# Two loads swapped between queues, and layernorm block 2 moved ahead of block 0, in the opening of a one-core attention and gMLP kernel

## The chip, the cores and the metric

The kernel runs on one core of a Trainium2 chip. The metric is device time in microseconds of one execution, taken as the median of several runs. A profiled execution has a time of its own and a span: from the first recorded instruction to the last. The core's engines run at the same time and each works through its own instructions in order: TensorE (PE; its weight loads are listed as PEld), VectorE (DVE), ScalarE (ACT), GpSimd (POOL) and SyncE (SP, here only an issuer of DMAs). ScalarE and GpSimd issue DMAs too. An instruction that needs another engine's result, or a transfer, waits for a semaphore, and everything behind it on its engine waits with it.

## The reference

Input x has 2048 rows of 512 values. It is normalized row by row, and two branches use the result: A, attention in which each position looks at 8 earlier ones two apart, and B, a gated MLP whose gate half z2 is normalized once more and mixed over the rows. The output is x plus both.

```python
def _B_ref(x, w_in, w_sp, b_sp, w_out):
    z = _gelu(jnp.einsum('bsd,df->bsf', x, w_in))     # w_in: 512 x 1792
    z1 = z[..., :Fh].copy()                           # Fh = 896
    z2 = _layernorm(z[..., Fh:], axis=-1)
    g = jnp.einsum('ts,bsf->btf', w_sp, z2) + b_sp[None, :, None]
    return jnp.einsum('bsf,fd->bsd', z1 * g, w_out)
x = A_x
xn = _layernorm(x, axis=-1)
return x + _A_ref(xn, A_wqkv, A_wo) + _B_ref(xn, B_w_in, B_w_sp, B_b_sp, B_w_out)
```

Only the opening of the kernel matters here: loading the first blocks of x and the z2 half of w_in, normalizing those blocks, transposing them, and the first z2 products.

## The kernel before

x is cut into 16 blocks of 128 rows. Each block goes through `ln_block`: VectorE takes statistics (`bnst`, L616, then `bnag`, L619), GpSimd turns the variance into a reciprocal root (`rstd`, L621), VectorE normalizes (`norm`, L631). For blocks 0 to 3 TensorE then transposes the block in two halves (`xTr..a` and `xTr..b`, L647), and ScalarE copies each half from PSUM to SBUF (`xTe..a`, `xTe..b`, L654). Blocks 4 and up are transposed by DMAs issued from SyncE (`xTd`, L635).

Block 0 has a shorter way. It is only centred, the second half by VectorE (`ctr1`, L624) and the first by ScalarE (`ctr0`, L626); the centred halves are transposed and used for its z2 product, and rstd0 is applied as the scale of the gelu. The normalized block 0 (`norm0`) is transposed separately for later use: `xNr` on TensorE (four transposes, L667) and `xNe` on ScalarE (L671). The first later user is Q0_0, the first product of the attention branch.

`z2_block` multiplies a transposed block with the z2 half of w_in, in two column halves of 448 (named 0 and 1, from the weights w2a and w2b); each column half is a sum over four chunks of the 512 inner values. For blocks 0 to 3 the sum is split into two tasks of two matmuls, `a` for the inner half 0 and `b` for the inner half 1 (z2_1_0a is block 1, column half 0, inner half 0; L824). ScalarE applies the gelu (`z2g`, L835). After z2 of blocks 0 to 3 come Q and K (L700), V (L682) and the rest; the DVE works on attention products from 17 us on.

The weights of z2 come in four loads of 224 KB (`ld_win_h`, L557): ldw_in2a_0, ldw_in2a_1, ldw_in2b_0 and ldw_in2b_1, where the last digit is the inner half. Each block of x is a load of 128 KB (`ld_x`, L547). Three loads of 512 KB follow for Q, K and V (ldq, ldk, L571; ldwv, L579).

A planner orders the tasks of each engine, but the openings are written out by hand in `plan.orders` (from L1061): one list for VectorE, one for ScalarE, one for SyncE, one for TensorE. In these lists an engine follows the text exactly. The loads of the opening are issued from two queues: SyncE issues ldx0, ldx1, ldw_in2a_0, ldw_in2b_0, ldx3 and others, ScalarE issues ldw_in2a_1, ldw_in2b_1 and ldx2. The loads ldx4, ldx5, ldx6, ldx7, ldq and ldk wait until ldw_in2b_1 has landed (`reads=[("w_in2b", 1)]`, `after=`). While TensorE waits for data at the very start it runs 28 small matmuls on constants (`warm`, L588).

Of the kernel before, what the change touches and what calls it, by code (L numbers as in the profile page):

```python
# [14 lines left out]
class Plan:  # L15
# [300 lines left out]
    warm=28,  # L316
    fill0=1,
# [4 lines left out]
def build_kernel(nc, A_x, A_wqkv, A_wo, B_x, B_w_in, B_w_sp, B_b_sp, B_w_out, out, report=False, sched_kw=None,  # L322
# [79 lines left out]
    with ExitStack() as es:  # L402
# [10 lines left out]
        def A(name, n, o2_=0):  # L413
            return ar[:, off[name] + o2_: off[name] + o2_ + n]

        def AC(o_, dims):
            return bass.AP(tensor=ar, offset=o_, ap=[[AR, 128]] + [list(d) for d in dims])
# [93 lines left out]
        def dma(eng, fn, nbytes, chan, reads=(), writes=(), name="", xbar=False, prio=None, lat=1700.0):  # L511
            return T(eng, fn, reads=tuple(reads), writes=tuple(writes), name=name, prio=prio,
                     dma=dict(chan=chan, nbytes=nbytes, xbar=xbar, lat=lat))
# [23 lines left out]
        def setup_masks():  # L537
            T("pool", lambda g: g.memset(maskt, 0.0), reads=[("rstd", 3)], writes=["maskt"], est=150, name="mask0", prio=2)
            mv = maskt.rearrange("p (w h) -> p w h", w=8)
            T("pool", lambda g: g.affine_select(out=mv, in_=mv, pattern=[[-2, 8], [0, 32]], compare_op=ALU.is_ge,  # L540
                                                fill=NEG_BIG, base=0, channel_multiplier=1),
              writes=["maskt"], est=400, name="mask1", prio=2)

        def xin_ap(sl):
            return A("xin", 512, 512 * sl) if sl < 4 else A("xin2", 512, 512 * (sl - 4))

        def ld_x(b, eng="sp", after=()):  # L547
            sl = b % 8
            dma(eng, lambda e: e.dma_start(xin_ap(sl), x2[128 * b:128 * b + 128, :]), 128 * 512 * 2,  # L549
                ("xin", sl), reads=after, writes=[("xin", sl)], name="ldx%d" % b)  # L550

        def ld_win(nm, lo, n, eng, after=()):
            dma(eng, lambda e: e.dma_start(AC(off["w_in"] + lo, [[1792, 4], [1, n]]),
                                           B_w_in[:, lo: lo + n].rearrange("(c p) n -> p c n", p=128)),
                512 * n * 2, nm, reads=after, writes=[nm], name="ld" + nm)

        def ld_win_h(nm, lo, n):  # L557
            for h in range(2):
                dma(("sp", "act")[h], (lambda h: lambda e: e.dma_start(  # L559
                    AC(off["w_in"] + lo + 2 * 1792 * h, [[1792, 2], [1, n]]),  # L560
                    B_w_in[256 * h: 256 * h + 256, lo: lo + n].rearrange("(c p) n -> p c n", p=128)))(h),
                    256 * n * 2, (nm, h), writes=[(nm, h)], name="ld%s_%d" % (nm, h))

        ld_x(0)
        ld_x(1)
        ld_win_h("w_in2a", FH, HF)
        ld_win_h("w_in2b", FH + HF, HF)
        ld_x(2, "act")
        ld_x(3, "sp")
        for which, eng in ((0, "sp"), (1, "sp")):  # L570
            dma(eng, (lambda which: lambda e: e.dma_start(  # L571
                AC(off["wqk"] + 512 * which, [[1024, 4], [1, 512]]),
                A_wqkv[:, 512 * which: 512 * which + 512].rearrange("(c p) n -> p c n", p=128)))(which),
                512 * 512 * 2, ("wqk", which), reads=[("w_in2b", 1)],
                writes=[(("wq", "wk")[which], c) for c in range(4)],
                name="ld%s" % ("qk"[which]))
        for b in range(4, min(8, NB)):
            ld_x(b, "sp", after=[("w_in2b", 1)])
        dma("sp", lambda e: e.dma_start(A("wv_raw", 2048).rearrange("p (c n) -> p c n", c=4),  # L579
                                        A_wqkv[:, 1024:1536].rearrange("(c p) n -> p c n", p=128)),  # L580
            512 * 512 * 2, "wv", writes=["wv_raw"], name="ldwv")
# [93 lines left out]
        def v_block(b):  # L675
            k = next_bank()
            sl = b % 4

            def mm(t):
                last = None  # L680
                for dc in range(4):
                    last = t.matmul(bank(k), AC(off["xnT"] + dc * S + 128 * b, [[1, 128]]),  # L682
                                    AC(off["wv_raw"] + 512 * dc, [[1, 512]]), start=(dc == 0), stop=(dc == 3))
                return last
            T("pe", mm, reads=[("xnT", b), "wv_raw"], writes=[("ps", k)], est=4 * c_mm(512), name="V%d" % b)
            T("act", lambda a: a.activation(A("Vn", 512, 512 * sl).rearrange("p (d h) -> p d h", d=16),
                                            bank(k).rearrange("p (h d) -> p d h", d=16), ACTF.Copy),
              reads=[("ps", k)], writes=[("Vn", sl)], est=c_act(512), name="Ve%d" % b)
            dma("pool", lambda e: e.dma_start(vscr[16 + 128 * b: 16 + 128 * b + 128, :], A("Vn", 512, 512 * sl)),
                128 * 512 * 2, ("vwr", sl), reads=[("Vn", sl)], writes=[("vscr", b)], name="Vw%d" % b)  # L690
# [165 lines left out]
        def z2_sq(b):  # L856
            T("act", lambda a: a.activation(A("sqj", FH), A("z2", FH, FH * b), ACTF.Square, accum_out=Fv("s2", 1, b)),  # L857
              reads=[("z2h", b, 0), ("z2h", b, 1)] + ([("z2h", 3, 1)] if b < 4 else []), writes=["sqj", ("s2", b), ("z2", b)],
              est=c_act(FH, psum=False, accum=True), name="z2s%d" % b)
# [30 lines left out]
        for j in range(NJ):  # L890
            bl = range(4 * j, 4 * j + 4)
            for b in bl:
                if b >= 8:
                    ld_x(b)
            if j == 1:
                ld_win("w_in1", 0, FH, "sp")
            if j == 0:
                for fn_, b, k0 in ((ln_block, 0, 3), (ln_block, 1, 1), (z2_block, 0, 5), (xn0_T, 0, 3), (ln_block, 2, 3), (z2_block, 1, 7),
                                   (z2_block, 2, 1), (ln_block, 3, 3), (z2_block, 3, 3)):
                    ring[0] = k0  # L900
                    fn_(b)
                setup_masks()
                dma("pool", lambda e: e.dma_start(vscr[0:16, :], ar[0:16, off["zeros"]: off["zeros"] + 512]), 16 * 512 * 2,
                    ("vwr", 0), reads=["zeros"], writes=[("vscr", -1)], name="Vzero", prio=2)
                ring[0] = 5
            else:
                for b in bl:
                    ln_block(b)
            if j == 1:
                dma("sp", lambda e: e.dma_start(A("bbc", S), bass.AP(tensor=B_b_sp.tensor, offset=B_b_sp.offset,  # L910
                                                                     ap=[[0, 128], [1, S]])),
                    128 * S * 2, "bbc", writes=["bbc"], name="ldbbc")
            if j >= 1:
                for b in bl:
                    v_block(b)
            for c in range(4):
                qk_pair(j, c)
            if j == 0:
                for b in bl:
                    v_block(b)  # L920
            prod_reduce(j)
            softmax(j)
            if j >= 1:
                for b in bl:
                    z2_block(b)
                for b in range(4 * (j - 1), 4 * j):
                    z2_sq(b)
                z2_wave(j - 1)
# [129 lines left out]
        for q in qord:  # L1058
# [1 line left out]

        plan.orders = [  # L1061
            """
                bnst0 bnag0 ctr1 bnst1 bnag1 norm0 norm1 bnst2 bnag2 bnst3 norm2 bnag3 bnst4 norm3 bnag4 bnst5 norm4
                bnag5 bnst6 norm5 bnag6 bnst7 norm6 bnag7
            """.split(),
            """
                actprime ldw_in2a_1 ldw_in2b_1 ldx2 ctr0 xTe0b xTe0a xTe1a xTe1b xNe z2g0_0 xTe2a xTe2b z2g0_1 z2g1_0
                xTe3a xTe3b z2g1_1 z2g2_0 z2g2_1 z2g3_0 z2g3_1
            """.split(),
            """  # L1070
                ldx0 ldx1 ldw_in2a_0 ldw_in2b_0 ldx3 ldx4 ldx5 ldq ldk ldx6 ldx7 ldwv
            """.split(),
            """
                warm xTr0b fill0 xTr0a z2_0_0b z2_0_1b z2_0_0a xTr1a xTr1b z2_0_1a xNr z2_1_0a z2_1_0b z2_1_1a xTr2a
                xTr2b z2_1_1b z2_2_0a z2_2_0b xTr3a xTr3b z2_2_1a z2_2_1b z2_3_0a z2_3_0b z2_3_1a z2_3_1b Q0_0 K0_0 Q0_1
                K0_1 Q0_2 K0_2 Q0_3 K0_3 V0 V1 V2 V3 V4 V5 V6 V7 Q1_0 K1_0 Q1_1 K1_1 Q1_2 K1_2 Q1_3 K1_3 z2_4_0 z2_4_1
                z2_5_0 z2_5_1 z2_6_0 z2_6_1 z2_7_0 z2_7_1 V8 V9 V10 V11 Q2_0 K2_0 Q2_1 K2_1 Q2_2 K2_2 Q2_3 K2_3 z2_8_0
                z2_8_1 z2_9_0 z2_9_1 z2_10_0 z2_10_1 z2_11_0 z2_11_1 V12 V13 V14 V15 Q3_0 K3_0 Q3_1 K3_1 Q3_2 K3_2 Q3_3
# [99 lines left out]
```

## Time and profile before

| What | us |
|---|---|
| median of 3 runs (lowest, highest) | 235.45 (235.31, 235.59) |
| the profiled execution's own time | 236.14 |
| its span | 233.8 |
| TensorE busy in the span | 229.3 (98%) |
| VectorE busy | 202.3 (87%) |
| ScalarE busy | 119.1 (51%) |
| GpSimd busy | 51.7 (22%) |

Busy times add up what an engine's instructions took; they do not say which engine sets the end. For that one reads the chain that ended last, followed back from the last instruction. In a timeline, a bracket at the end of a line tells how long the engine had been idle before the instruction and what released it. DMAs are seen twice: as an issue on the queue of the engine that issues them (SPq, ACTq), and as packets on a hardware queue, q1 for those of SyncE and q10 for those of ScalarE.

### The profile page before, as it was taken

To read this page: it belongs to the slowest core of one execution; us is meant where nothing else is said; L and a number is where in the kernel's file an instruction comes from. 1 tells how busy PE (TensorE), PEld (TensorE's weight loads), DVE (VectorE), ACT (ScalarE), POOL (GpSimd) and SP (SyncE) were. 2 spreads that over 40 slices of the span, in tenths; PEclk is the share of its full clock that TensorE was granted. 3 is DMA by queue.
4 is the path that set the end of the run, shared out by engine and by line. 5 is a ranking of instruction groups with operands and counts; after the bars stand their busy time and mean duration, and the time that the engine had idled before them with its cause. 6 is when DMAs were issued, how large, how long until landed. Compare 5 with 4: busy or idle time off the path is not lost.

```text
span 233.8 us, 2996 instructions
## 1 busy us (share of the span) xinstructions
PE 229.3 (98%) x1108; PEld 112.7 (48%) x1127; DVE 202.3 (87%) x230; ACT 119.1 (51%) x235; POOL 51.7 (22%) x69
## 2 busy tenths in 40 slices
PE   8999999999999999999999999999999999999996
PEld 6554455554554444444444444444444444444544
DVE  4769979998989989997999998999999999999200
ACT  4789588989988978952021124341232415101442
POOL 4548964680780050001201000010000000000000
PEclk9999999999999999999999999999999999999999
DMA  6897850399909999681429999999829794920412
GB/s 220 271 251 173 188 139 3 103 196 330 353 32 179 216 238 267 121 231 51 141 78 276 252 167 246 229 323 292 265 53 260 138 251 108 227 44 7 112 48 67
DMA packets 87166, 41.76 MB, mean 179 GB/s; under 512 B 66272, under 2 KB 86000, under 8 KB 87152
## 3 DMA queue, kind: packets, MB, share of 16 engines
q1 hardware_dynamic: 71072, 23.24, 47.8%
q10 hardware_dynamic: 14640, 14.13, 21.0%
q0 software_dynamic: 1440, 4.21, 6.3%
q8 instruction: 9, 0.15, 0.3%
q14 instruction: 5, 0.04, 0.1%
HBM read 20.05 MB, written 5.26 MB: 108 GB/s over the span
## 4 chain that ended last, share of the span: by engine, by line
PE 96%; DMA 2%; issue 1%; SPq 1%; ACT 0%
PE ps L959 41%; PE ps L700 12%; PE ps L1029 10%; PE ps L847 10%; PE ps L824 10%; PE ps L1025 6%; PE ps L682 6%; DMA arena<-in_B_w_in_dram 2%; SPq L549 0%; PE ps L647 0%; SPq L559 0%; ACT arena L1038 0%; PE ps L667 0%
## 5 line engine op out<-in xcount | busy, mean ns | idle before, releaser
L959 PE MATMUL ps<-arena 128*128 128x512 bf16 x440 | 97.1, 379 | 0.4
L959 PEld LDWEIGHTS ps<-arena 128*128 128x128 bf16 x448 | 43.8, 98 | 52.8
L953 ACT ACTIVATE ps<-arena 128x512 f32<-128x512 bf16 x28 | 16.5, 599 | 48.5 <-DVE arena L966 47.8
L984 DVE TENSOR_TENSOR arena<-arena 128x4096 bf16<-128x4096 bf16 x16 | 36.3, 2284 | 0.4
L724 DVE TENSOR_TENSOR arena<-arena 128x4096 bf16<-128x4096 bf16 x16 | 36.1, 2280 | 0.1
L988 DVE TENSOR_TENSOR arena<-arena 128x4096 bf16<-128x4096 bf16 (+1 forms) x16 | 28.0, 1753 | 0.3
L700 PE MATMUL ps<-arena 128*128 128x512 bf16 x127 | 28.1, 379 | 0.1
L729 DVE TENSOR_TENSOR arena<-arena 128x4096 bf16<-128x4096 bf16 x12 | 27.4, 2287 | 0.2
L1029 PE MATMUL ps<-arena 128*128 128x512 bf16 (+2 forms) x123 | 26.8, 355 | 0.2
L824 PE MATMUL ps<-arena 128*128 128x448 bf16 x128 | 25.8, 353 | 0.3 <-ACT arena L654 0.2
L1038 ACT ACTIVATE arena<-ps 128x512 bf16<-128x512 f32 (+2 forms) x17 | 9.5, 561 | 29.6 <-PE ps L1029 29.6
L847 PE MATMUL ps<-arena 128*128 128x512 bf16 x109 | 24.0, 379 | 0.2
L700 PEld LDWEIGHTS ps<-arena 128*128 128x128 bf16 x128 | 14.5, 113 | 13.1
L966 DVE TENSOR_TENSOR arena<-ps,arena 128x512 bf16<-128x512 f32 x28 | 19.1, 681 | 0.6 <-PE ps L959 0.6
L1029 PEld LDWEIGHTS ps<-arena 128*128 128x128 bf16 x126 | 13.6, 113 | 11.0
L708 ACT ACTIVATE arena<-ps 128x1024 bf16<-128x1024 f32 x16 | 16.4, 1022 | 3.1 <-PE ps L700 2.5
L824 PEld LDWEIGHTS ps<-arena 128*128 128x128 bf16 x128 | 12.0, 98 | 11.9 <-ACT arena L654 1.2
L852 ACT ACTIVATE arena<-ps 128x512 bf16<-128x512 f32 x28 | 16.0, 595 | 3.2 <-PE ps L847 2.7
L835 ACT ACTIVATE arena<-ps 128x448 bf16<-128x448 f32 x30 | 16.2, 552 | 2.3 <-issue 0.3
L847 PEld LDWEIGHTS ps<-arena 128*128 128x128 bf16 x112 | 10.9, 98 | 13.2
L1025 PE MATMUL ps<-arena 128*128 128x512 bf16 (+2 forms) x71 | 16.7, 355 | 0.1
L857 ACT ACTIVATE arena<-arena 128x896 bf16<-128x896 bf16 x16 | 15.1, 944 | 0.0
(68 smaller groups left out, 195.5 us busy)
## 6 DMA issues: line engine op xcount, KB each, us to landing
arena<-vscr ACTq DMA_DIRECT2D x8, 1152.0 KB, 9.2
arena<-in_A_x_dram ACTq DMA_DIRECT2D x17, 128.0 KB, 5.9
vscr<-arena POOLq DMA_DIRECT2D x16, 128.0 KB, 2.5
arena<-in_A_x_dram SPq DMA_DIRECT2D x15, 128.0 KB, 2.9
out_dram<-arena ACTq DMA_DIRECT2D x15, 128.0 KB, 1.9
arena<-in_A_wqkv_dram SPq DMA_DIRECT2D x3, 512.0 KB, 5.8
ascr<-arena POOLq DMA_DIRECT2D x4, 256.0 KB, 5.1
arena<-ascr POOLq DMA_DIRECT2D x4, 256.0 KB, 4.0
```

Of the source, the lines that this page charges most:

```text
L700: last = t.matmul(bank(k + which), AC(off["wqk"] + 1024 * dc + col0, [[4, 128]]), AC(off["xnT"] + dc * S + 512 * j, [[1, 512]]), start=(dc ...
L724: T("dve", lambda v: v.tensor_tensor(pbv, qb, kb, ALU.mult), reads=[("QT", c, j), ("KT", c, j), ("KTpad", c, j)], writes=[("pb", s_)], est ...
L729: T("dve", lambda v: v.tensor_tensor(A("pb", 4096, 4096 * a), A("pb", 4096, 4096 * a), A("pb", 4096, 4096 * b), ALU.add), reads=[("pb", b) ...
L824: last = t.matmul(ps[:, 512 * k: 512 * k + HF], st, AC(off["w_in"] + 1792 * dc + c0, [[1, HF]]), start=(h == first and dc == 2 * h), stop= ...
L847: lastm = t.matmul(bank(k), AC(off["w_in"] + 1792 * dc + 128 * fc, [[1, 128]]), AC(off["xnT"] + dc * S + 512 * j, [[1, 512]]), start=(dc = ...
L953: T("act", lambda a: a.activation(bank(k), A("bbc", 512, 512 * tc), ACTF.Copy), reads=["bbc"], writes=[("ps", k)], est=c_act(512), name="g ...
L959: last = t.matmul(bank(k), AC(off["z2"] + FH * sh + 128 * fc, [[1, 128]]), AC(off["wT"] + WSL * r_ + sh * 512, [[1, 512]]), start=False, s ...
L966: T("dve", lambda v: v.tensor_tensor(uv, bank(k), uv, ALU.mult), reads=[("ps", k)], writes=[("z1T", fc, tc)], est=c_dve(512) + 20, name="u ...
L984: T("dve", (lambda iv, tv, av: lambda v: v.tensor_tensor(tv, iv, av, ALU.mult))(iv, tv, av), reads=[("attn", j), ("Ve", par)], writes=[("V ...
L988: T("dve", (lambda n: lambda v: v.tensor_tensor(AC(off["Vs"], [[4096, 2], [1, n]]), AC(off["Vs"], [[4096, 2], [1, n]]), AC(off["Vs"] + n, ...
L1025: t.matmul(po, AC(off["OT"] + 512 * ot_pos(tb) + 128 * cc, [[1, 128]]), AC(off["wo"] + 512 * cc + c0, [[1, n]]), start=False, stop=False, ...
L1029: last = t.matmul(po, AC(off["z1T"] + fc * S + t0, [[ts, 128]]), AC(off["w_out"] + 512 * fc + c0, [[1, n]]), start=False, stop=(fc == FC - ...
```

## The change

Three things change, all in the opening.

The loads: ldx1 moves from SyncE to the head of ScalarE's loads, and ldw_in2a_1 moves from there to the second place of SyncE's. The loads that waited for ldw_in2b_1 wait for ldw_in2a_0 instead.

VectorE's order: bnst2 moves ahead of norm1, norm2 ahead of bnst3, and norm0 from before norm1 to after bnag3.

TensorE's and ScalarE's order: the four transposes of the normalized block 0 (xNr) move from before z2_1 to before z2_3, and their copy (xNe) from before z2g0_0 to after z2g1_0. Some halves of z2_1 and the transposes of block 2 change places, and xNr gets another PSUM bank.

```diff
         def ld_win_h(nm, lo, n):
             for h in range(2):
-                dma(("sp", "act")[h], (lambda h: lambda e: e.dma_start(
+                dma("act" if h and nm == "w_in2b" else "sp", (lambda h: lambda e: e.dma_start(
...
         ld_x(0)
-        ld_x(1)
+        ld_x(1, "act")
...
-                512 * 512 * 2, ("wqk", which), reads=[("w_in2b", 1)],
+                512 * 512 * 2, ("wqk", which), reads=[("w_in2a", 0)],
...
-            ld_x(b, "sp", after=[("w_in2b", 1)])
+            ld_x(b, "sp", after=[("w_in2a", 0)])
...
-                for fn_, b, k0 in ((ln_block, 0, 3), (ln_block, 1, 1), (z2_block, 0, 5), (xn0_T, 0, 3), (ln_block, 2, 3), (z2_block, 1, 7),
+                for fn_, b, k0 in ((ln_block, 0, 3), (ln_block, 1, 1), (z2_block, 0, 5), (xn0_T, 0, 5), (z2_block, 1, 7), (ln_block, 2, 3),
...
-                bnst0 bnag0 ctr1 bnst1 bnag1 norm0 norm1 bnst2 bnag2 bnst3 norm2 bnag3 bnst4 norm3 bnag4 bnst5 norm4
+                bnst0 bnag0 ctr1 bnst1 bnag1 bnst2 norm1 bnag2 norm2 bnst3 bnag3 norm0 norm3 bnst4 bnag4 bnst5 norm4
...
-                actprime ldw_in2a_1 ldw_in2b_1 ldx2 ctr0 xTe0b xTe0a xTe1a xTe1b xNe z2g0_0 xTe2a xTe2b z2g0_1 z2g1_0
-                xTe3a xTe3b z2g1_1 z2g2_0 z2g2_1 z2g3_0 z2g3_1
+                actprime ldx1 ldw_in2b_1 ldx2 ctr0 xTe0b xTe0a xTe1a xTe1b z2g0_0 xTe2a xTe2b z2g0_1 xTe3a xTe3b z2g1_0
+                xNe z2g1_1 z2g2_0 z2g2_1 z2g3_0 z2g3_1
...
-                ldx0 ldx1 ldw_in2a_0 ldw_in2b_0 ldx3 ldx4 ldx5 ldq ldk ldx6 ldx7 ldwv
+                ldx0 ldw_in2a_1 ldw_in2a_0 ldw_in2b_0 ldx3 ldx4 ldx5 ldq ldk ldx6 ldx7 ldwv
...
-                warm xTr0b fill0 xTr0a z2_0_0b z2_0_1b z2_0_0a xTr1a xTr1b z2_0_1a xNr z2_1_0a z2_1_0b z2_1_1a xTr2a
-                xTr2b z2_1_1b z2_2_0a z2_2_0b xTr3a xTr3b z2_2_1a z2_2_1b z2_3_0a z2_3_0b z2_3_1a z2_3_1b Q0_0 K0_0 Q0_1
+                warm xTr0b fill0 xTr0a z2_0_0b z2_0_1b z2_0_0a xTr1a xTr1b z2_0_1a z2_1_0a z2_1_0b xTr2a xTr2b z2_1_1a
+                z2_1_1b z2_2_0a z2_2_0b xTr3a xTr3b z2_2_1a z2_2_1b xNr z2_3_0a z2_3_0b z2_3_1a z2_3_1b Q0_0 K0_0 Q0_1
```

## The prediction, made before the changed kernel ran

> **What bounds the kernel now.** I read the page first, then the chain that ended last from the start to 14 us, then the timelines of TensorE, VectorE and ScalarE up to 14 us, and last the DMA view in short stretches. Page and chain:
>
> ```profile
> span 233.8 us, 2996 instructions
> ...
> PE   8999999999999999999999999999999999999996
> ...
> PE 96%; DMA 2%; issue 1%; SPq 1%; ACT 0%
> ```
>
> ```profile
> 2.12 4.87 DMA arena<-in_B_w_in_dram
> 6.99 0.05 issue
> 7.04 0.55 PE ps L824 x2
> 7.59 0.22 PE ps L667 x4
> 7.81 1.14 PE ps L824 x6
> ```
>
> In the slices TensorE is full from the second to the last but one. In the chain everything after 7.04 us is matmul, with pieces of 0.05 us between: the rest of the span is a fixed queue of TensorE work of 224 us, and it can only start earlier or later. At 7.04 TensorE was waiting for a weight transfer issued at 2.12, which is w2b0 (ldw_in2b_0; w2a and w2b are the two column halves of the z2 weights, 0 and 1 their row halves; x0 to x7 are the blocks of x). So only the first 8 us can change the time, unless the change opens a hole later.
>
> What TensorE and ScalarE do there (start, length, engine, line):
>
> ```profile
> 5.37 1.37 PE L824 MATMUL ps<-arena 128*128 128x448 bf16 x6 [0.21 <-ACT arena L654]
> 6.58 0.39 PE L647 MATMUL ps<-arena 128*128 128x128 bf16 x4
> 6.89 0.66 ACT L654 ACTIVATE arena<-ps 128x256 bf16<-128x256 f32 x2 [1.29 <-PE ps L647]
> 7.04 0.55 PE L824 MATMUL ps<-arena 128*128 128x448 bf16 x2
> 7.42 0.39 PE L667 MATMUL ps<-arena 128*128 128x128 bf16 x4
> ```
>
> Six z2 matmuls at 0.19 us each (the chain's 1.14 for six) plus four transposes at 0.22 in all are 1.36 us of work, between 5.37 and 7.04. So 1.67 - 1.36 = 0.31 us of it is idle, and that is all that the loads and the order can win after 5.37 (0.13% of 235.45). The start at 5.37 hangs on x0 alone: landing, statistics at 3.19, centring at 4.16, transposes, copy.
>
> VectorE's order of the same time:
>
> ```profile
> 4.36 0.69 DVE L616 BATCH_NORM_STATS2 fpool<-arena 128x6 f32<-128x512 bf16 x1
> 5.08 0.20 DVE L619 BATCH_NORM_AGGREGATE fpool<-fpool 128x2 f32<-128x9 f32 x1
> 5.19 0.37 DVE L631 TENSOR_SCALAR arena<-arena,fpool 128x512 bf16<-128x512 bf16 x1
> 6.02 0.41 DVE L631 TENSOR_SCALAR arena<-arena,fpool 128x512 bf16<-128x512 bf16 x1 [0.46 <-POOL fpool L621]
> 6.42 0.69 DVE L616 BATCH_NORM_STATS2 fpool<-arena 128x6 f32<-128x512 bf16 x1
> ```
>
> These are bnst1, bnag1, norm0, norm1 (it waited 0.46 us for GpSimd's rstd1) and bnst2. The DMA view, cut to the issue of x2 and to two stretches of half a microsecond (2.75 to 3.25, and 5.5 to 6; queue, packets, MB):
>
> ```profile
> arena<-in_A_x_dram ACTq DMA_DIRECT2D x1, 128.0 KB, 4.5
> ```
>
> ```profile
> q10 hardware_dynamic: 177, 0.15, 90.2%
> q1 hardware_dynamic: 28, 0.03, 15.6%
> ```
>
> ```profile
> q1 hardware_dynamic: 204, 0.18, 102.6%
> q10 hardware_dynamic: 16, 0.01, 8.3%
> ```
>
> The first says that x2, issued at 1.87, landed 4.5 us later, at 6.37. Cutting the view around each issue gives the others: x0 issued 0.73, landed 3.1; w2a1 0.86, 3.8; x1 1.18, 4.1; w2b1 1.35, 5.65; w2a0 1.65, 6.05; x2 1.87, 6.37; w2b0 2.12, 7.0; x3 2.63, 7.3. The landings come in the order of issue over both queues, and in the two stretches one queue has nearly all the traffic although the other has a transfer waiting: x1, issued at 1.18 on SyncE's queue q1, hardly moves at 2.75 to 3.25, while ScalarE's q10 carries weights issued earlier.
>
> **The change part by part.** *The loads.* x1 goes to the head of ScalarE's queue, issued near 0.86 for 1.18; w2a1 takes its place on SyncE's, 1.18 for 0.86. Nothing is added: SyncE still issues twelve loads, ScalarE three. The six other loads of the opening keep their issue times, since each queue holds as many issues ahead of them (some 0.45 us each). x1 earlier is worth nothing: bnst1 at 4.36 follows ctr1 on VectorE without a wait, and x1 was there at 4.1. w2a1 in x1's old slot lands at 4.1 to 4.6 (96 KB more at 340 KB a microsecond is 0.3), needed at 5.37: nothing. The Trainium skill, "DMA: Bandwidth & Descriptors", Issuing engines are not separate DMA queues, says that loads from several engines interleave on the same 16 DMA engines and that a second issuer saves only issue time; that speaks against a gain, and the 0.32 us by which x1 is issued earlier is then all there is, which nobody waits for.
>
> *The DMA waits on SyncE.* ldx4, ldx5, ldq and ldk wait for w2a0 (6.05) instead of w2b1 (5.65), and ldx6, ldx7 and ldwv queue behind: each up to 0.4 us later. wk, the closest one, lands at 7.0 + 5.8 = 12.8 and is wanted by K0_0 at 13.01 + 4 x 0.216 (the chain: 6.91 us for 32) = 13.9; 13.2 still does. x6 (bnst6 waited for it until 13.14) then makes VectorE some 0.4 us later up to the first product at 17.07; VectorE ends its chain of work at 218, 14 us before the end, so this is covered. Without that cover it would cost up to 0.4.
>
> *bnst2 ahead of norm1.* This is the step that decides. VectorE runs in order: bnag1, bnst2, norm1. bnst2 cannot start before x2 lands, and norm1 is queued behind it; behind norm1 stand the transposes of block 1 on TensorE, and behind those z2_0_1a and everything else. Let L be x2's landing. bnst2 starts at L + 0.05 (as 6.42 after 6.37), norm1 0.62 later (bnst3 at 7.39 to norm2 at 8.01, the same pair without a dependence), and lasts 0.41. The transposes' weight load follows 0.06 after it (6.43 to 6.49), ScalarE's copy 0.40 after that (6.49 to 6.89), and the first weight load of z2_1 0.44 after the copy starts (9.09 to 9.53 in block 2, 4.93 to 5.37 in block 0), with 0.05 to its matmul. So z2_1 starts at L + 0.05 + 0.62 + 0.41 + 0.06 + 0.40 + 0.44 + 0.05 = L + 2.03, against 7.81 now. z2_0_1a (two matmuls, 0.38) fits behind the transposes before that.
>
> *xNr later.* Block 0's four transposes (0.22) leave the place before z2_1, where they were already done by 7.81, and come back unchanged before z2_3: the same 0.22 in TensorE's queue. At the old place they covered the copy of block 1; now the wait above stands open. Shift of the end = L + 2.03 - 7.81 + 0.22 = L - 5.56.
>
> *The rest of the order.* Carried on with the same steps for L = 6.2, norm2 ends near 8.5 and the transposes of block 2 are due at 9.0; norm3 (now behind norm2, bnst3, bnag3, norm0) ends near 10.4, due 10.7; xNe ends near 12.7, and Q0_0, which needs it, is due at 13.6. No new hole, but the second and third are 0.3 and 0.9 us deep, no more.
>
> *What L is.* No row shows x2 behind x1 and w2b1. If loads are served in order of issue, the same 928 KB as now is ahead of it (only x1 and w2a1 change places): L = 6.37, shift +0.81. If the queues share evenly, ScalarE's has 480 KB up to the end of x2 instead of 576; 96 KB at half of 365 GB/s is 0.54 us: L = 5.83, shift +0.27. The traffic rows (one queue at a time) lie nearer to the first, so I take L = 6.2: shift +0.64. Span 233.8 + 0.64 = 234.4. The profiled execution took 236.14, 0.69 above the median of the runs, 235.45; the same shift on the median gives **236.1**.
>
> **The rivals.** *Even sharing*: +0.27, 235.7. For it: landings in the order of issue would follow here too, since the queues hold like amounts. Against it: x1 at a standstill at 2.75 to 3.25. The Trainium skill, same page, Queues, rings and completion order, says that each DMA engine takes turns between the queues it has work for, packet by packet; by that rule this case would hold, and the two stretches shown do not agree with it.
>
> *Not slower*: x2 lands while VectorE would idle anyway, by 5.35, so that bnst2 disappears in the wait for rstd1. norm1 then stays at 6.02, z2_1 could start at 6.02 + 0.41 + 0.06 + 0.40 + 0.44 + 0.05 = 7.38, and behind w2b0 at 7.04 + 0.38 = 7.42: shift 7.42 - 7.81 + 0.22 = -0.17, 235.3. The point that decides is L = 5.56. Against it: it needs x2 a full microsecond earlier, with only 96 KB less ahead of it in its queue. If x0 landed 0.3 us earlier as well, because the transfer beside it is smaller (128 for 224 KB), -0.5 would come out: 234.95. Nothing shows that the neighbour slows x0, which is issued first.
>
> *A second hole*: x2 lands as late as 6.5, and norm3 or xNe uses up its margin, 0.2 more: 0.94 + 0.2 = +1.14, 236.6. For it: norm0 and norm3 are now one chain behind x2. Against it: each had 0.3 us or more left.
>
> **How the numbers follow.** L from 6.03 up to about 6.45 (shift +0.47 to +0.9): 0.58. Second hole: 0.06. Even sharing: 0.26. Not slower: 0.06, and with an earlier x0 0.04. 0.2% is 0.47 us, about what a measurement of this kernel can tell from no change. So slower 0.58 + 0.06 = 0.64, same 0.26 + 0.06 = 0.32, faster 0.04. The range reaches from the low end of even sharing less the 0.14 us by which the runs of before scatter (L = 5.65: 235.45 + 0.09 - 0.14 = 235.4) to the forecast's top end and the same scatter (236.5).
>
> **What would show it.** Right: VectorE idles after bnag1 (5.28) until bnst2, released by the DMA of x at about 6.25; norm1 near 6.9; TensorE has a hole of some 0.8 us before the block 1 transposes at 7.34; from z2_1 on it is full, all later pieces 0.5 to 0.8 us late. Wrong: bnst2 right behind bnag1; a hole ended by a weight transfer instead; or holes after 9 us.

## The result, and the profile after

The changed kernel is slower: 236.36 us median of 21 runs, against 235.48 for the kernel before, also 21. The ratio is 1.0033, with a 95% interval of 1.0024 to 1.0042: +0.78 us (0.57 to 0.99), at 235.45 us for the whole; the two medians lie 0.88 apart. The forecast was +0.64 us and 236.1, with a range of 235.4 to 236.5.

From the page of the changed kernel: span, TensorE's slices, and the chain that ended last by engine.

```profile
span 234.7 us, 2996 instructions
...
PE   8899999999999999999999999999999999999996
...
PE 95%; DMA 2%; issue 0%; DVE 0%; ACT 0%; ACTq 0%
```

Only the second slice of TensorE (5.9 to 11.7 us) has changed, from 9 to 8, so the loss is to be looked for there. The chain that ended last, its first pieces in order of time (start, length, what):

```profile
1.76 4.92 DMA arena<-in_A_x_dram
6.68 0.02 issue
6.70 0.69 DVE fpool L616
7.39 0.33 DVE arena L631
7.72 0.05 issue
7.77 0.40 PE ps L647 x4
8.16 1.29 PE ps L824 x6
```

Before, the piece ahead of the matmuls was the load of w2b0. Now it is the load of x2, followed on VectorE by bnst2 (L616) and norm1 (L631), and on TensorE by the transposes of block 1 (L647). VectorE's and TensorE's timelines show the same from the other side (start, length, engine, line; in the bracket the idle time before and its releaser):

```profile
5.03 0.20 DVE L619 BATCH_NORM_AGGREGATE fpool<-fpool 128x2 f32<-128x9 f32 x1
6.70 0.69 DVE L616 BATCH_NORM_STATS2 fpool<-arena 128x6 f32<-128x512 bf16 x1 [1.48 <-DMA arena<-in_A_x_dram]
7.31 0.40 DVE L631 TENSOR_SCALAR arena<-arena,fpool 128x512 bf16<-128x512 bf16 x1
```

```profile
5.38 0.93 PE L824 MATMUL ps<-arena 128*128 128x448 bf16 x4
6.92 0.55 PE L824 MATMUL ps<-arena 128*128 128x448 bf16 x2 [0.61 <-DMA arena<-in_B_w_in_dram]
7.77 0.40 PE L647 MATMUL ps<-arena 128*128 128x128 bf16 x4 [0.29 <-DVE arena L631]
8.00 1.46 PE L824 MATMUL ps<-arena 128*128 128x448 bf16 x6
...
11.03 0.39 PE L647 MATMUL ps<-arena 128*128 128x128 bf16 x4
```

bnag1 is done at 5.23 and VectorE then stands still for 1.48 us until x2 lands; norm1 waits behind it and runs at 7.31 instead of 6.02. But TensorE stopped twice: 0.61 us for w2a0, which landed at 6.87 instead of 6.05, then 0.29 us for norm1. The first wait was not forecast; a hole ended by a weight transfer stood among the signs that the forecast would be wrong. After 8 us there is no further hole above 0.2 us.

For comparing profiles I use the start of block 3's transposes, the last L647 line: 10.30 before, 11.03 now. TensorE before, from z2_1 (7.65) on:

```profile
7.65 1.30 PE L824 MATMUL ps<-arena 128*128 128x448 bf16 x6
...
10.30 0.39 PE L647 MATMUL ps<-arena 128*128 128x128 bf16 x4
```

In the old order xNr (0.22 us) lies ahead of it, in the new order behind it, so the shift of all that follows is 11.03 - 10.30 + 0.22 = 0.95. The spans, 234.7 and 233.8, say 0.9.

### The profile page after: what moved, and what is told of

It reads as the page before. It is cut to its first block, busy times and chain, and to the rows that moved or that the text cites. A ratio compares the mean times of both kernels' runs of the same rounds, so it can differ in the third digit from the quotient of the medians.

```text
span 234.7 us, 2996 instructions
## 1 busy us (share of the span) xinstructions
PE 229.5 (98%) x1108; PEld 112.7 (48%) x1127; DVE 202.4 (86%) x230; ACT 119.1 (51%) x235; POOL 51.6 (22%) x69
## 4 chain that ended last, share of the span: by engine, by line
PE 95%; DMA 2%; issue 0%; DVE 0%; ACT 0%; ACTq 0%
PE ps L959 41%; PE ps L700 12%; PE ps L1029 10%; PE ps L847 10%; PE ps L824 10%; PE ps L1025 6%; PE ps L682 6%; DMA arena<-in_A_x_dram 2%; PE ps L647 0%; DVE fpool L616 0%; ACT L594 0%; ACTq L559 0%; DVE arena L631 0%; ACT arena L1038 0%; PE ps L667 0%
```

## The experiments

Two theories went in. A: norm1 waiting behind bnst2 for x2 is the cost, and the new loads are free. B: the new loads themselves make weights late, and TensorE's wait for w2a0 is a cost of its own. All times are against the kernel before on the same chip; a ratio is turned into microseconds with 235.45.

**The loads alone.** The kernel before, with the loads and their waits of the change:

```diff
-                dma(("sp", "act")[h], (lambda h: lambda e: e.dma_start(
+                dma("act" if h and nm == "w_in2b" else "sp", (lambda h: lambda e: e.dma_start(
...
-        ld_x(1)
+        ld_x(1, "act")
...
-                actprime ldw_in2a_1 ldw_in2b_1 ldx2 ctr0 ...
+                actprime ldx1 ldw_in2b_1 ldx2 ctr0 ...
...
-                ldx0 ldx1 ldw_in2a_0 ldw_in2b_0 ldx3 ...
+                ldx0 ldw_in2a_1 ldw_in2a_0 ldw_in2b_0 ldx3 ...
```

> Only the loads of the change; every compute order as before. Theory A (norm1 waiting behind bnst2 for x2 is the cost; the loads by themselves cost nothing): norm1 at about 6.0 us, within 0.15 us of before in time. Theory B (the loads by themselves make the weights late: in the changed kernel the first row half of the first z2 weights landed at 6.9 us instead of 6.05, and TensorE waited for it): the third pair of z2 matmuls starts at about 6.9, the block 1 transposes behind it at 7.3, z2_1 at about 8.05 instead of 7.65, so 0.4 to 0.5 us slower than before.

Measured: ratio 1.0008 (0.9999 to 1.0017), +0.19 us (-0.02 to +0.40). Its profile, TensorE:

```profile
6.98 0.55 PE L824 MATMUL ps<-arena 128*128 128x448 bf16 x2 [0.82 <-DMA arena<-in_B_w_in_dram]
7.37 0.39 PE L647 MATMUL ps<-arena 128*128 128x128 bf16 x4
```

In this profile B's steps are all there: w2a0 at 6.9, the transposes at 7.4, and the span 234.3, 0.5 us longer. The execution that was profiled took 236.16, the median of all is 235.68, and the interval holds A's answer and just reaches the lower end of B's. So the loads can hold TensorE up, but that they cost something in the typical run is not settled by this.

**The orders alone.** The kernel before, with VectorE's, ScalarE's and TensorE's new orders:

```diff
-                bnst0 bnag0 ctr1 bnst1 bnag1 norm0 norm1 bnst2 bnag2 bnst3 norm2 bnag3 bnst4 norm3 ...
+                bnst0 bnag0 ctr1 bnst1 bnag1 bnst2 norm1 bnag2 norm2 bnst3 bnag3 norm0 norm3 bnst4 ...
...
-                ... xTr1a xTr1b z2_0_1a xNr z2_1_0a z2_1_0b z2_1_1a xTr2a
+                ... xTr1a xTr1b z2_0_1a z2_1_0a z2_1_0b xTr2a xTr2b z2_1_1a
```

> Only the compute orders of the change; the loads and their waits as before. Theory A: x2 lands at 6.37 as before, bnst2 starts there, norm1 at 7.0, the block 1 transposes at 7.45; the changed kernel had 6.7, 7.31, 7.77 and was 0.95 us late from there on, so here 0.6 to 0.7 us slower than before. Theory B: with the weights at their old times the order alone costs little, 0 to 0.3 us.

Measured: 1.0013 (1.0003 to 1.0023), +0.31 us (0.07 to 0.54). x2 landed at 6.07 in its profile, earlier than the 6.37 that the expectation took over. VectorE waited for it all the same, and TensorE for norm1:

```profile
6.10 0.69 DVE L616 BATCH_NORM_STATS2 fpool<-arena 128x6 f32<-128x512 bf16 x1 [0.58 <-DMA arena<-in_A_x_dram]
```

```profile
7.16 0.40 PE L647 MATMUL ps<-arena 128*128 128x128 bf16 x4 [0.35 <-DVE arena L631]
...
10.43 0.39 PE L647 MATMUL ps<-arena 128*128 128x128 bf16 x4
```

The new order costs something with the old loads too, and through the wait that A names; the size follows the landing (10.43 - 10.30 + 0.22 = 0.35). It is less than the 0.6 to 0.7 that A gave, and the landing accounts for that too: 0.30 us earlier than the 6.37 that A reckoned with. Between this kernel and the changed one only the loads and their waits differ, and the timed runs tell the two apart: +0.31 (0.07 to 0.54) with the old loads, +0.78 (0.57 to 0.99) with the new. So the new loads put some half a microsecond on top of the new order, more than the 0.19 us that they cost under the old order.

**norm1 first.** The changed kernel, with one pair put back:

```diff
-                bnst0 bnag0 ctr1 bnst1 bnag1 bnst2 norm1 bnag2 ...
+                bnst0 bnag0 ctr1 bnst1 bnag1 norm1 bnst2 bnag2 ...
```

> The changed kernel with norm1 back ahead of bnst2 on VectorE, nothing else. Theory A: norm1 at 6.0, the block 1 transposes ready at 6.5; most of the loss goes, time within 0.2 us of before. Theory B: the transposes stand behind z2_0_0a, which waits for weights until 6.9, so they start at 7.3 and z2_1 at 8.05: 0.4 to 0.5 us slower than before, about half of the loss left.

Measured: 1.0024 (1.0015 to 1.0032), +0.57 us (0.35 to 0.75). A's "within 0.2 us" falls. norm1 ran at 6.00, but z2_0_0a stood at 6.94 for w2a0, as B said, and then came a second wait. TensorE's weight loads, and VectorE:

```profile
10.85 0.23 PEld L647 LDWEIGHTS ps<-arena 128*128 128x128 bf16 x4 [0.54 <-DVE arena L631]
```

```profile
10.32 0.47 DVE L631 TENSOR_SCALAR arena<-arena,fpool 128x512 bf16<-128x512 bf16 x1 [0.44 <-POOL fpool L621]
```

That is block 3's transposes waiting for norm3. In the new order bnst3 stands behind norm2, and norm2 needs x2, so the late block reaches TensorE a second time: x2, bnst2, norm2, bnst3, rstd3, norm3 in one line. TensorE was done with its earlier work (eight matmuls from 9.07 on, 0.19 us each) at 10.6 and idled 0.25 us. Putting norm1 back takes away the wait for norm1, but neither of the other two. Of these, the chain that ended last goes through norm3 back to x2 (landed at 6.73) and not through w2a0: with w2a0 in time, block 3's transposes would still have waited for norm3.

**x2 second on ScalarE.** The changed kernel, with x2 issued ahead of w2b1:

```diff
-                actprime ldx1 ldw_in2b_1 ldx2 ctr0 ...
+                actprime ldx1 ldx2 ldw_in2b_1 ctr0 ...
```

> The changed kernel with x2 issued second on ScalarE, ahead of w2b1. Theory A: x2 lands by about 5, bnst2 follows bnag1 at 5.3 without a wait, norm1 at 6.0; shift against before between -0.2 and +0.1 us. Theory B: the wait for x2 is gone, but z2_0_0a still waits for w2a0 at about 6.9 (and z2_0_1b for w2b1 at about 5.6): 0.4 to 0.5 us slower than before.

Measured: 1.0073 (1.005 to 1.0096), +1.7 us (1.2 to 2.3). Both theories miss. x2 came in time, bnst2 ran at 5.04 without a wait, but w2b1 now landed at 7.21, where the changed kernel had it at 4.8 and theory B reckoned with 5.6, and z2_0_1b, second in TensorE's z2 order, stood for it:

```profile
7.25 0.93 PE L824 MATMUL ps<-arena 128*128 128x448 bf16 x4 [1.42 <-DMA arena<-in_B_w_in_dram]
```

The span of this profile is 235.0, against a median of 233.6 for the timed runs of the kernel before: 1.4 us. Of the six runs two had a granted TensorE clock of 0.993, where every other run listed has 0.999 or 1.0, and took 238.07 and 237.90; the median of the other four is 236.8, 1.4 us above the 235.45 of the kernel before. So about 0.3 of the 1.7 goes with those two runs; why their clock was lower is open.

**The old wait of the later loads.** The changed kernel, with ldx4 to ldx7, ldq and ldk waiting for w2b1 again:

```diff
-                512 * 512 * 2, ("wqk", which), reads=[("w_in2a", 0)],
+                512 * 512 * 2, ("wqk", which), reads=[("w_in2b", 1)],
...
-            ld_x(b, "sp", after=[("w_in2a", 0)])
+            ld_x(b, "sp", after=[("w_in2b", 1)])
```

> The changed kernel, but ldx4 to ldx7, ldq and ldk wait for w2b1 again, as before. In the changed order of loads w2b1 lands at 4.8 and w2a0 at 6.9, so they are issued about 2 us earlier. Theory A and B: nothing on the path waits for them and they stand behind x3 on SyncE's queue; x2 lands at 6.6 to 6.8 as in the changed kernel, and the time is that of the changed kernel within 0.2 us, 0.7 to 0.9 us slower than before. Theory C (the new wait is part of the loss, by x6 and the Q and K weights coming later): at least 0.3 us of the loss goes.

Measured: 1.0033 (1.0021 to 1.0045), the ratio of the changed kernel itself. The new wait is no measurable part of the loss, and theory C falls. The profile is useful for another reason: here w2a0 landed at 6.2, so that TensorE stood for it only from 5.92 to 6.24 (four matmuls of 0.19 us from 5.16 on, then the hole), x2 at 6.7, and still block 3's transposes started where they did in the changed kernel:

```profile
6.74 0.69 DVE L616 BATCH_NORM_STATS2 fpool<-arena 128x6 f32<-128x512 bf16 x1 [1.64 <-DMA arena<-in_A_x_dram]
```

```profile
7.80 0.40 PE L647 MATMUL ps<-arena 128*128 128x128 bf16 x4 [1.01 <-DVE arena L631]
...
11.06 0.39 PE L647 MATMUL ps<-arena 128*128 128x128 bf16 x4
```

**Filling the hole of the kernel before.** The kernel before, with xNr in the wait for w2b0:

```diff
-                ... z2_0_0a xTr1a xTr1b z2_0_1a xNr z2_1_0a ...
+                ... z2_0_0a xTr1a xTr1b xNr z2_0_1a z2_1_0a ...
```

> The kernel before with one edit on TensorE: the four transposes of the normalized block 0 go ahead of z2_0_1a instead of behind it, into the 0.24 us in which TensorE waited for w2b0 before 7.04. If that hole is idle time, z2_1 starts at 7.4 instead of 7.65 and the time is 0.15 to 0.22 us less than before, about 0.09%, at the edge of what 5 rounds can tell. If the copy of block 1 sets z2_1 instead, the gain is under 0.1 us.

Measured: 1.0006 (0.9992 to 1.0021): no gain, and one of 0.09% just outside the interval. In its own profile w2b0 landed at 6.6 and not at 7.0, and the next run shows the same.

**Second profiles of both kernels, unchanged.**

> The kernel before, unchanged, for a second profile of its loads. If the order of loads sets when x2 and w2a0 land: 6.0 to 6.4 and 5.5 to 6.1. If it is chance from run to run: anywhere from 5.5 to 7.

> The changed kernel, unchanged, for a second profile of its loads. If the order of loads sets when x2 and w2a0 land: 6.6 to 6.8 and 6.8 to 7.0, as in the three profiles with these loads so far. If it is chance: anywhere from 5.5 to 7.

The second profile of the kernel before has hardly a hole: its block 1 transposes from 6.67 on, 0.22 us of work, are through at 6.89, and z2_0_1a follows at 6.91, because w2b0 landed at 6.7 instead of 7.0:

```profile
6.67 0.40 PE L647 MATMUL ps<-arena 128*128 128x128 bf16 x4
6.91 0.54 PE L824 MATMUL ps<-arena 128*128 128x448 bf16 x2
```

So the 0.31 us between 5.37 and 7.04 was partly the luck of the first profile, and an edit that fills it has little to win. The second profile of the changed kernel, VectorE and TensorE:

```profile
6.19 0.69 DVE L616 BATCH_NORM_STATS2 fpool<-arena 128x6 f32<-128x512 bf16 x1 [1.04 <-DMA arena<-in_A_x_dram]
```

```profile
7.25 0.40 PE L647 MATMUL ps<-arena 128*128 128x128 bf16 x4 [0.43 <-DVE arena L631]
...
10.52 0.39 PE L647 MATMUL ps<-arena 128*128 128x128 bf16 x4
```

x2 landed here at 6.17, half a microsecond before any other profile with these loads, and w2a0 at 6.2; TensorE's weight load waited for that until 6.26, which was over long before norm1. So neither expectation holds whole: the landings scatter, and the order of loads moves them. The shift between two single profiles scatters with them: 0.95 from the first pair, 10.52 - 10.16 + 0.22 = 0.58 from the second (10.16 is the same line in the second profile of before). Their mean is 0.77, against 0.78 in the timed runs.

Put together, four profiles have the new orders whole, two of the changed kernel, one each with the old loads and the old wait. From the start of bnst2 to block 3's transposes they give 11.03 - 6.70 = 4.33, 10.52 - 6.19 = 4.33, 10.43 - 6.10 = 4.33 and 11.06 - 6.74 = 4.32 us. In these four TensorE's timetable hangs on x2's landing and nothing else, over a spread of 0.6 us in that landing, and whether or not w2a0 was late as well.

## Why the prediction was right

*The bound.* Right: TensorE has no hole above 0.2 us from 8 us on in both kernels, and the shift made in the opening stays in the span to the end (0.95 and 0.9).

*bnst2 ahead of norm1.* Right, and it is what sets the end. The forecast said a shift of L - 5.56 with L the landing of x2. The four profiles, with bnst2 0.02 us after the landing, give L + 0.02 + 4.33 - 10.30 + 0.22 = L - 5.73. The 0.17 us between the two constants are what is left of three errors. First, z2_1 started at 8.53 (its weight load, below, at 8.52), 1.85 us behind x2's 6.68 and not 2.03: each step of the sum was given a little too long, most of all the copy, which came 0.33 and not 0.40 us after the weight load. Second, the forecast set this against 7.81, the chain's time for z2_1, while the timeline, from which its steps are read, has 7.65. These two, 0.18 and 0.16, cancel by luck. The third is a place that the forecast did not follow. In the old order TensorE's weight load for z2_2_0a waited 0.42 us for ScalarE's copy of block 2, which opened a hole of 0.15 us ahead of block 3's transposes. In the new order the same wait stands ahead of z2_1, where the forecast has it in its sum, and z2_1_1 as a whole covers the copy of block 2, so that the later hole is gone. The weight loads, before and then in the changed kernel:

```profile
9.53 0.12 PEld L824 LDWEIGHTS ps<-arena 128*128 128x128 bf16 x2 [0.42 <-ACT arena L654]
```

```profile
8.52 0.11 PEld L824 LDWEIGHTS ps<-arena 128*128 128x128 bf16 x2 [0.42 <-ACT arena L654]
```

*What L is.* This is the term that was mis-sized, the other way. The forecast took 6.2, between 6.37 (service in order of issue) and 5.83 (even sharing). With the new loads and compute orders, x2 landed at 6.68, 6.71 and 6.17, a mean of 6.5; with the loads of the change but other compute orders at 6.8 and 6.7. The old loads gave 6.37, 6.07, 5.95 and 6.26. So the new loads made x2 later by some 0.4 us on the mean, where one reading had no change and the other a gain, although x2 was issued 0.1 us earlier (1.76 for 1.87). The reading in order of issue lost its premise as well: w2a0 is issued ahead of x2 in both kernels and landed ahead of it in all four profiles with the old loads, but behind it in three of five with the new, and level with it in a fourth. That the number came out so close is in part luck, since the two errors nearly cancel: 6.5 - 5.73 = 0.77, against 0.78 measured. With the 10.16 of the second profile of before in place of 10.30 it would be 0.91.

*The loads cost nothing.* Only half right. Their new wait costs nothing measurable, as argued and as the fifth experiment shows. But w2a0, which the forecast had at an unchanged 6.05, landed at 6.9 in three of the six profiles with the new loads in their full or nearly full form (6.2 to 6.75 in the others). In the changed kernel this wait lies inside the longer wait for norm1; in its second profile it is down to 0.25 us. With norm1 put back it shows again, but there norm3 sets the start of what follows.

*The rest of the order.* "No new hole" holds for the changed kernel. But the margin of norm3, given as 0.3 us, was used up in its profile: norm3 ends at 10.92, the transposes' weights load from 10.98 on, and the transposes start at 11.03, just when TensorE comes free (9.52 + 8 x 0.19 = 11.04). This is the rival of the second hole as far as its condition goes; it cost nothing here, and it is the wait that the experiment with norm1 first brought out.

*The rivals.* Even sharing needed x2 at 5.83; no profile with the change's order of loads had it before 6.17. The rule of the Trainium skill that stood beside it ("DMA: Bandwidth & Descriptors", Queues, rings and completion order: turns between the queues, packet by packet) does not show here as an even split in time. In the first profile of the changed kernel q1 and q10 moved 0.01 and 0.16 MB from 3.75 to 4.25 us and 0.16 and 0.02 from 5.25 to 5.75; but between, from 4.25 to 5.25, it was 0.20 and 0.11, so one queue at a time does not hold throughout either. "Not slower" needed x2 by 5.56; moving x2 forward in its queue did bring it in time (4.7), and cost more by w2b1 than it saved.

## What to carry to other kernels

Where an engine runs strictly in order, an instruction that needs a late transfer should stand behind all work that is ready and that others wait for: one statistics pass moved ahead of a ready normalization handed the landing of a load straight to the bound engine. When the DMA engines are full, changing the place of one load in a queue moves the others by half a microsecond or more; cost such an edit with every load behind it at its new landing, not only with the one that is moved. And take the landings from more than one profile before counting on a hole of a few tenths.

## What the runs showed of the hardware

The landing of one and the same load, in one and the same kernel, moved by half a microsecond between two profiles (x2 at 6.68 and 6.17 in the changed kernel; w2a0 at 6.87 and 6.2). And the order of issue had an effect that the bytes don't explain. With x1 and w2a1 exchanged between the queues, the fifth and sixth load, with the same bytes issued ahead of them, landed later: w2a0 at 6.2 to 6.93 instead of 5.55 to 6.05, x2 at 6.17 to 6.77 instead of 5.95 to 6.37. The fourth, w2b1, did not: 4.7 to 5.1 instead of 4.95 to 5.65.

Part of this can be seen in the traffic. From 1.75 to 4.25 us the DMA engines moved the same in both kernels (0.70 and 0.71 MB). From 4.25 to 5.75 they moved less with the new loads; before, and then the changed kernel:

```profile
DMA packets 640, 0.55 MB, mean 367 GB/s; under 512 B 45, under 2 KB 640, under 8 KB 640
```

```profile
DMA packets 562, 0.49 MB, mean 325 GB/s; under 512 B 35, under 2 KB 562, under 8 KB 562
```

In the four profiles with the old loads this mean is 353 to 372 GB/s, in the five with the loads of the change 306 to 350. The last packets come later too: ScalarE's queue still moved 17 packets from 5.75 to 6.25 us and one after that, against 9 and none before. Why the traffic slows down and its tail grows with the new loads was not tried and stays open.
